# Planning TensorE ahead of ScalarE's next scores, with VectorE's tiles placed by a table, in a fused attention and routed-MLP kernel

## The chip, the cores and the metric

The kernel runs on one core of one Trainium2 chip. The metric is the device time of one execution in microseconds. Before is given by three timed runs, and by one profiled execution of which page and trace are quoted.

## The reference

An attention layer with 16 query heads and one key and value head, then a layer that routes 8 of the 2048 tokens through a gated MLP. D is 448, a head 28 wide, the MLP 1792.

```python
x = A_x                                    # (1, 2048, 448), bfloat16
h = x + attention(layernorm(x))            # q = x wq, k = x wk, v = x wv, softmax(q k / sqrt(28)) v wo
n = layernorm(h)
r = n @ w_r; idx = top 8 of r              # over the 2048 tokens
y = (silu(n[idx] @ w_gate) * (n[idx] @ w_up)) @ w_down * sigmoid(r[idx])
return h + n + scatter(y, idx)
```

## The kernel before

**Blocks and tiles.** The attention is cut into 16 blocks: block b is query block b // 4 (512 queries) for the four heads of group b % 4. Each block has 16 key tiles j of 128 keys. A tile has 4 x 512 x 128 scores, in two halves p of two heads. One half is a *score pair*: two 64-row matmuls side by side on TensorE (`qk`, ps<-Q,K), into two PSUM banks of 512 columns.

**Two ways to the exponential.** Most tiles are ScalarE's (`act_unit`): the score pair goes to banks 0 and 1 or 2 and 3 in turn, and one ACTIVATE of 128 x 1024 (line L982) writes P, a ring of six places. Four matmuls with the values (`act_pv`, ps<-P,Vs, the *value product*) then use two places, that is one tile. The other tiles are VectorE's (`dve_unit`): the pair goes to banks 4 and 5, a clamp to integers (L994) makes the bits of a bfloat16, and after both halves three shifted copies of the tile (`shift`, L1001) give, with four scaled sets of values, a finer exponential; each of the four has its own value product (`dve_pv`, ps<-Y,Vs). A shift takes either VectorE or, for tiles in `shared`, its third one GpSimd. 63 of the 256 tiles are VectorE's.

**Banks.** Block b adds its value products up in bank 6 + b % 2. The other of banks 6 and 7 serves, during block b, the query projection of block b + 2 (`q_project`, ps<-xnT,wq_pad, then a copy to Q) and the rows of the output projection (`out_proj`, ps<-wo_pad,On). When a block is done, VectorE copies the bank to Ot (`post_block`, L715); only then may block b + 2 begin its value products there, and block b + 1's projections use it. The sums of the softmax then go through DRAM for a reciprocal, and GpSimd makes On.

**Start and end.** The tokens come in four chunks of 512. `chunk0` and `chunk` normalize, transpose (ps<-ident,xn) and project keys and values; blocks 0 and 1 run interleaved while the later chunks are made. `late_consts` fills constants that are needed later, on GpSimd. After the last exponential come the last block's division, the last four rows of 128 tokens, the choice of the 8 tokens and their MLP.

**What sets the order.** All work is first recorded as operations with an engine, an estimated duration, dependencies and a priority (`_Graph.op`). `_Graph.plan` then plays the engines on a time line of these estimates: each engine takes, of its operations that are ready, the one with the lowest priority number, and if none is ready the one that will be ready first. The resulting orders are emitted as they are, with semaphores; on the chip each engine works through its own in that order. Priorities are places in the sequence of blocks, 16 to a block: ScalarE's score pairs get `t - 3`, VectorE's `t - 2.9`, chunk c `8 * c - 3`. VectorE's tiles per block come from short hand-made lists (`where`, `LD`, `FD`), the shared shifts from `PN`, and the query projections stand at 6.5 sixteenths of each block.

Of the kernel before, what the change touches and what calls it, by code (L numbers as in the profile page):

```python
# [15 lines left out]

PE, AC, DV, PO, SP = "pe", "act", "dve", "pool", "sp"


class _Op:  # L20
    __slots__ = ("eng", "fns", "dur", "lat", "deps", "prio", "idx", "dma", "start", "end", "sig", "name", "nsucc",
                 "pred_left", "succs", "ready", "form", "lock")


class _Graph:
# [16 lines left out]
    def op(self, eng, fns, dur, reads=(), writes=(), prio=None, dma=False, acc=False, name="", form=0,  # L42
           after=(), lock=False):
        o = _Op()
# [7 lines left out]
        o.form = form  # L52
        o.lock = (lock or eng == PO) and not dma
# [30 lines left out]
    def plan(self):  # L84
# [180 lines left out]
def _main(nc, G, sb, ps, psb, flag, scr, xs, ptab, A_x, A_wq, A_wk, A_wv, A_wo, B_w_r, B_w_gate, B_w_up, B_w_down, out,  # L265
# [156 lines left out]
    dma(wk_sb[0:CK, :, :], A_wk.rearrange("(k p) n -> p k n", p=CK), ["wk_sb"], lat=4450.0)  # L422
    dma(wq_sb[0:CK, :, 0:CK], wq_v[:, :, 0:CK], [("wq", 0)], lat=5300.0)
    dma(wv_sb[0:CK, :, :], A_wv.rearrange("(k p) n -> p k n", p=CK), ["wv_sb"], lat=5700.0)
    dma(wq_sb[0:CK, :, CK:D], wq_v[:, :, CK:D], [("wq", 1)], lat=6400.0)
# [25 lines left out]
    def pad_wq(g, after=()):  # L451
# [5 lines left out]
        else:  # L457
# [39 lines left out]
    def late_consts(gate):  # L497
        G.prio = -400
        G.op(PO, lambda e: e.tensor_copy(wv_pad[0:CK, :, 1:1 + DH], wv_sb[0:CK, :, :]), 250,
             reads=["wv_sb", "wv_pad"], writes=["wv_pad"], after=gate)  # L500
# [5 lines left out]
        for i in range(4):  # L506
# [13 lines left out]
        G.op(PO, lambda e: e.iota(iota_i[:, 0, 0:4], [[128, 4]], base=8, channel_multiplier=1), 140, writes=["iota_i"], after=gate)  # L520
        G.op(PO, lambda e: e.iota(iota_i[:, 0, 4:5], [[0, 1]], base=0, channel_multiplier=1), 140, writes=["iota_i"], after=gate)
        G.op(PO, lambda e: e.tensor_copy(iota_n[:, :], iota_i[:, 0, 0:5]), 200, reads=["iota_i"], writes=["iota_n"])
        G.op(PO, lambda e: e.iota(iota_i[:, 1, 0:1], [[0, 1]], base=0, channel_multiplier=128), 140, writes=["iota_j"], after=gate)
        G.op(PO, lambda e: e.tensor_copy(p128[:, :], iota_i[:, 1, 0:1]), 200, reads=["iota_j"], writes=["p128"])
        G.op(PO, lambda e: e.iota(idi[0:8, 0:96], [[1, 96]], base=0, channel_multiplier=0), 250, writes=["idi"], after=gate)
        G.op(PO, lambda e: e.tensor_copy(iota96[:, :], idi[0:8, 0:96]), 300, reads=["idi"], writes=["iota96"])
        G.op(PO, lambda e: e.iota(iota_i[:, 0, :], [[256, NT // 2], [0, 2]], base=0, channel_multiplier=0), 140,
             writes=["iota_i"], after=gate)
        G.op(PO, lambda e: e.iota(iota_i[:, 1, :], [[0, NT // 2], [128, 2]], base=0, channel_multiplier=1), 140,
             writes=["iota_i", "iota_j"], after=gate)  # L530
# [3 lines left out]
        G.op(PO, lambda e: e.iota(idi[:, :], [[-32, 4], [0, 32]], base=0, channel_multiplier=1), 250, writes=["idi"], after=gate)  # L534
# [782 lines left out]
```

## Time and profile before

| | |
|---|---|
| three timed runs | 393.46 us median, 392.99 to 394.96 |
| the profiled execution | 392.07 us, its span 390.2 us |
| busiest engines | ScalarE 375.1 us, TensorE 348.8, VectorE 344.1, GpSimd 117.2 |
| moved by DMA | 17.12 MB in all, 44 GB/s |

The page's busy shares are averages. With several engines near 90% it is the holes in the row of one engine, and what stands ahead of the late instruction, that tell the bound; the timeline and the chain show these. Matmul ends in the trace are modelled, so starts are the safer numbers. "PE" is TensorE, "DVE" VectorE, "ACT" ScalarE, "POOL" GpSimd, and all TensorE matmuls but transposes have one line (L400), so that they are told apart by their tiles.

### The profile page before, as it was taken

To read this page: it belongs to the slowest core of one execution; us is meant where nothing else is said; L and a number is where in the kernel's file an instruction comes from. 1 tells how busy PE (TensorE), PEld (TensorE's weight loads), DVE (VectorE), ACT (ScalarE), POOL (GpSimd) and SP (SyncE) were. 2 spreads that over 40 slices of the span, in tenths; PEclk is the share of its full clock that TensorE was granted. 3 is DMA by queue.
4 is the path that set the end of the run, shared out by engine and by line. 5 is a ranking of instruction groups with operands and counts; after the bars stand their busy time and mean duration, and the time that the engine had idled before them with its cause. 6 is when DMAs were issued, how large, how long until landed. Compare 5 with 4: busy or idle time off the path is not lost.

```text
span 390.2 us, 8159 instructions
## 1 busy us (share of the span) xinstructions
PE 348.8 (89%) x3373; PEld 108.8 (28%) x3373; DVE 344.1 (88%) x617; ACT 375.1 (96%) x431; POOL 117.2 (30%) x150
## 2 busy tenths in 40 slices
PE   8899889999888998989988999999898998999945
PEld 7344222222222222222222222222222222222225
DVE  6985879999998999989998999988999998999482
ACT  6999989999999999999999999999999999999992
POOL 7440000540145020444145342543402254212100
PEclk9899999999999999999999999999999999999985
DMA  8696000100000000010102000010102010111011
GB/s 210 157 235 185 2 2 1 46 16 26 5 7 25 3 28 27 30 47 16 40 6 73 2 29 27 29 47 17 41 3 77 3 52 26 40 37 34 0 50 54
DMA packets 18045, 17.12 MB, mean 44 GB/s; under 512 B 6660, under 2 KB 15124, under 8 KB 18004
## 3 DMA queue, kind: packets, MB, share of 16 engines
q1 hardware_dynamic: 17652, 16.32, 14.5%
q8 instruction: 27, 0.44, 0.5%
q10 hardware_dynamic: 288, 0.23, 0.2%
q14 instruction: 14, 0.11, 0.1%
q0 software_dynamic: 64, 0.02, 0.0%
HBM read 11.70 MB, written 4.86 MB: 42 GB/s over the span
## 4 chain that ended last, share of the span: by engine, by line
ACT 74%; PE 19%; DVE 5%; issue 1%; POOL 0%; POOLq 0%
ACT P L982 73%; PE ps L400 18%; DVE Y L994 2%; DVE Y L1001 1%; ACT xn L928 1%; PE ps L403 1%; DVE bn L898 0%; ACT x_sb L789 0%; POOL out_dram L1209 0%; ACT Rb L705 0%; ACT Rb L703 0%; DVE Ot L715 0%; POOL ident L430 0%; DVE On L709 0%; ACT wq_sb L1206 0%
## 5 line engine op out<-in xcount | busy, mean ns | idle before, releaser
L982 ACT ACTIVATE P<-ps 128x1024 bf16<-128x1024 f32 x386 | 357.1, 1093 | 4.8 <-PE ps L400 3.9
L400 PE MATMUL ps<-Q,K 64*128 64x512 bf16 x1024 | 181.7, 386 | 28.1 <-ACT P L982 20.4
L994 DVE TENSOR_SCALAR Y<-ps 128x1024 int16<-128x1024 f32 x126 | 153.2, 1216 | 16.4 <-PE ps L400 15.8
L1001 DVE TENSOR_SCALAR Y<-Y 128x2048 int16<-128x2048 int16 x155 | 104.9, 702 | 0.6
L400 PEld LDWEIGHTS ps<-Q,K 64*128 64x128 bf16 x1024 | 45.0, 93 | 171.5 <-ACT P L982 132.7
L1001 POOL TENSOR_SCALAR Y<-Y 128x2048 int16<-128x2048 int16 x34 | 64.5, 1899 | 84.1 <-DVE Y L1001 78.8
L400 PE MATMUL ps<-Y,Vs 128*32 128x512 bf16 x1008 | 86.9, 383 | 0.5 <-DVE Y L1001 0.2
L400 PE MATMUL ps<-P,Vs 128*32 128x512 bf16 x772 | 76.4, 389 | 0.5 <-DVE Vs L487 0.3
L400 PEld LDWEIGHTS ps<-Y,Vs 128*32 128x32 bf16 x1008 | 24.9, 95 | 31.2 <-issue 18.9
L400 PEld LDWEIGHTS ps<-P,Vs 128*32 128x32 bf16 x772 | 19.8, 93 | 42.3 <-issue 40.5
L731 POOL TENSOR_TENSOR On<-Ot,Rb 128x512 bf16<-128x512 f32 x15 | 19.1, 1272 | 36.1 <-DVE Y L1001 16.3
L727 POOL TENSOR_TENSOR Ls<-Ls,Lc 128x16 f32<-128x16 f32 x15 | 3.3, 220 | 77.3 <-DVE Y L1001 59.6
L400 PE MATMUL ps<-xnT,wq_pad 112*128 112x512 bf16 (+1 forms) x68 | 18.7, 371 | 0.4 <-DVE Ot L715 0.4
L400 PE MATMUL ps<-wo_pad,On 128*128 128x448 bf16 (+1 forms) x64 | 17.0, 358 | 1.5 <-DVE On L709 1.3
L479 DVE TENSOR_SCALAR Q<-ps,qone 128x512 bf16<-128x512 f32 x15 | 11.1, 737 | 2.4 <-PE ps L400 2.4
L759 POOL TENSOR_TENSOR hbuf<-st,nhalf 128x1 f32<-128x1 f32 x12 | 7.5, 627 | 17.6 <-DVE Y L1001 10.9
L715 DVE COPY Ot<-ps 128x512 f32<-128x512 f32 x15 | 10.2, 683 | 1.1 <-PE ps L400 0.8
L725 POOL TENSOR_TENSOR Lsi<-Lsi,Li 128x16 f32<-128x16 f32 x15 | 4.0, 266 | 17.1 <-DVE Y L1001 11.8
L753 DVE TENSOR_TENSOR hbuf<-ps,x_sb 128x448 f32<-128x448 f32 x12 | 7.4, 618 | 1.0 <-PE ps L400 0.8
L1209 POOL DMA_INDIRECT out_dram<-wq_sb,idxc x1 | 0.9, 931 | 24.2 <-DVE wq_sb L1208 24.2
L768 DVE SCALAR_TENSOR_TENSOR junk<-hbuf,w_rb 128x448 bf16<-128x448 f32 x12 | 8.1, 678 | 0.0
L755 DVE BATCH_NORM_STATS2 bn<-hbuf 128x6 f32<-128x448 f32 x12 | 7.5, 623 | 0.2
(209 smaller groups left out, 174.1 us busy)
## 6 DMA issues: line engine op xcount, KB each, us to landing
Rb<-h_scr SPq DMA_DIRECT2D x15, 256.0 KB
h_scr<-hbuf SPq DMA_DIRECT2D x12, 225.0 KB, 2.2
out_dram<-x_sb SPq DMA_DIRECT2D x8, 224.0 KB, 2.1
wg_sb<-in_B_w_gate_dram SPq DMA_DIRECT2D x1, 1568.0 KB, 11.9
wu_sb<-in_B_w_up_dram SPq DMA_DIRECT2D x1, 1568.0 KB, 18.2
wd_sb<-in_B_w_down_dram SPq DMA_DIRECT2D x1, 1568.0 KB, 21.9
x_sb<-in_A_x_dram SPq DMA_DIRECT2D x3, 448.0 KB, 5.7
wo_pad<-in_A_wo_dram SPq DMA_DIRECT2D x4, 98.0 KB
```

Of the source, the lines that this page charges most:

```text
L400: return lambda e: e.matmul(o, lhsT=l, rhs=r, start=start, stop=stop)
L479: G.op(DV, lambda e: e.tensor_scalar(Q[:, b % 4, :], ps[:, bank, :], qone[:, 0:1], None, ALU.add), dvt(512), reads=[pk(bank), "qone"], wri ...
L715: G.op(DV, lambda e: e.tensor_copy(Ot[:, rb, :], ps[:, acc_bank(b), :]), dvt(512), reads=[pk(acc_bank(b))], writes=[("Ot", rb)], prio=u - 30)
L725: G.op(LE, lambda e: e.tensor_tensor(Lsi[:, :], Lsi[:, :], Li[:, rb, :], ALU.add), 150, reads=["Lsi", ("Li", rb)], writes=["Lsi"])
L731: G.op(PO, lambda e: e.tensor_tensor(On[:, qb % 2, g, :], Ot[:, rb, :], Rb[:, rb, :], ALU.mult), 1270, reads=[("Ot", rb), ("Rb", rb)], wri ...
L753: G.op(DV, lambda e: e.tensor_tensor(h, ps[:, bank, 0:D], x_sb[:, t, 0:D], ALU.add), dvt(D), reads=[pk(bank), ("x", t)], writes=[("h", hr)])
L755: G.op(DV, lambda e: e.bn_stats(bn6[:, t, :], h), dvt(D), reads=[("h", hr)], writes=[("bn6", t)])
L759: G.op(PO, lambda e: e.tensor_tensor(s4, st[:, t, 7:8], nhalf[:, 0:1], ALU.pow), 570, reads=[("st7", t), "nhalf"], writes=[("h4", hr)])
L768: G.op(DV, lambda e: e.scalar_tensor_tensor(junk[:, :], h, s4, w_rb[:, :], ALU.mult, ALU.mult, accum_out=st[:, t, 2:3]), 700, reads=[("h", ...
L982: marks["exp"] = G.op(AC, lambda e: e.activation(P[:, sl, :, :], ps[:, b0:b0 + 2, :], ACT.Exp, bias=EBIAS, scale=OCT), 905, reads=[pk(b0), ...
L994: G.op(DV, lambda e: e.tensor_scalar(Y[:, n, 0, p:p + 3:2, :].bitcast(I16), ps[:, 4:6, :], 0.0, 32639.0 - 3 * STEP, ALU.max, ALU.min), 114 ...
L1001: G.op(PO if po else DV, lambda e: e.tensor_scalar(Y[:, n, v, :, :].bitcast(I16), Y[:, n, 0, :, :].bitcast(I16), 1.0, v * STEP, ALU.mult, ...
```

## The change

The planner gets a flag `crit`, set on ScalarE's score pairs. When TensorE is about to take another operation and such a pair will be ready soon, it takes only work that ends within SLACK (248 ns) of that moment; if there is none and the pair is less than WAIT (240 ns) away, TensorE is left idle for it. The lists for VectorE's tiles are replaced by a table: per block the tiles, how many shifts go to GpSimd, and an offset of their times; four early tiles in blocks 0 and 1 (before: five); a place for each query projection, output row and chunk. 62 tiles are VectorE's. The planning latencies of four DMAs are lowered, the wv_pad copy stands with the first constants, and the iotas lose their dependence on the first chunk.

```diff
+SLACK, WAIT = 248.0, 240.0
+TILES = {
+    2: ((0, 5, 8, 13), 4, -0.95),
+    3: ((0, 3, 6, 10, 13), 3, 0.94),
...
+EARLY = [(0, 5, 18.21), (0, 15, 22.04), (0, 4, 23.54), (1, 12, 28.01)]
+QUERY = {2: 12.3, 3: 12.3, 4: 6.9, 5: 7.0, 6: 11.5, 7: 11.1, 8: 8.7, 9: 10.4, 10: 6.7, 11: 9.5, 12: 10.1, 13: 7.6}
+ROWS = {
+    (0, 0): 10.9, (0, 1): 7.3, (0, 2): 10.3, (0, 3): 9.3, (1, 0): 10.7, (1, 1): 11.9, (1, 2): 13.1,
+    (1, 3): 9.9, (2, 0): 6.2, (2, 1): 11.4, (2, 2): 8.4, (2, 3): 9.2
+}
+CHUNK = (0.0, 5.1, 10.9, 36.9)
@@ plan
                 if now:
                     c = min(now, key=lambda o: (o.prio, o.idx))
                     s = t
+                    soon = min((o for o in lst if o.crit and t < o.ready), key=lambda o: o.ready, default=None)
+                    if soon is not None and not c.crit and c.eng == PE:
+                        fit = [o for o in now if t + o.dur + 100.0 * (o.form != form) <= soon.ready + SLACK]
+                        if fit:
+                            c = min(fit, key=lambda o: (o.prio, o.idx))
+                        elif soon.ready - t < WAIT:
+                            c, s = soon, soon.ready
@@ _main
-    dma(wk_sb[0:CK, :, :], A_wk.rearrange("(k p) n -> p k n", p=CK), ["wk_sb"], lat=4450.0)
+    dma(wk_sb[0:CK, :, :], A_wk.rearrange("(k p) n -> p k n", p=CK), ["wk_sb"], lat=3300.0)
...
+    G.op(PO, lambda e: e.tensor_copy(wv_pad[0:CK, :, 1:1 + DH], wv_sb[0:CK, :, :]), 250,
+         reads=["wv_sb", "wv_pad"], writes=["wv_pad"])
@@ late_consts
-        G.op(PO, lambda e: e.tensor_copy(wv_pad[0:CK, :, 1:1 + DH], wv_sb[0:CK, :, :]), 250,
-             reads=["wv_sb", "wv_pad"], writes=["wv_pad"], after=gate)
-        G.op(PO, lambda e: e.iota(iota_i[:, 0, 0:4], [[128, 4]], base=8, channel_multiplier=1), 140, writes=["iota_i"], after=gate)
+        G.op(PO, lambda e: e.iota(iota_i[:, 0, 0:4], [[128, 4]], base=8, channel_multiplier=1), 140, writes=["iota_i"])
...
@@ chunk
-        G.prio = 8 * c - 3.0
+        G.prio = CHUNK[c]
@@ tiles
-    groups = [5 if b in (5, 10) else 3 if b in () else 4 for b in range(NB)]
-    PN = {2: 3, 4: 5, 6: 3, 7: 2, 8: 5, 9: 3, 10: 5, 11: 5, 13: 5, 14: 2}
-    LD = (0, 3, 7, 10)
-    FD, FN, FT, FS = (5, 9, 13), 5, 18.5, 2.8
-    where = {0: (), 1: (9,), 2: (5, 11), 3: (3, 7, 11), 4: (1, 5, 9, 13), 5: (1, 4, 7, 10, 13)}
...
-        d = where[groups[b]] if b < NB - 1 else LD
+        d, _, dt = TILES[b]
         for j in range(NT):
             if j in d:
-                dve_tiles.append((b, j, 16.0 * b + j - 0.5))
+                dve_tiles.append((b, j, 16.0 * b + j - 0.5 + dt))
...
-    shared = {m for m, (b, j, t) in enumerate(dve_tiles) if rank[m] < PN.get(b, 0)}
+    shared = {m for m, (b, j, t) in enumerate(dve_tiles) if b in TILES and rank[m] < TILES[b][1]}
...
         G.op(PE, qk(b0, b, j, p), 216, reads=[("Q", b % 4), ("Qh", b % 4), kk(j, p)], writes=[pk(b0), pk(b0 + 1)],
-             prio=t - 3, form=1)
+             prio=t - 3, form=1, crit=True)
...
-            at(16 * b + 6.5, q_project, b + 2, misc_bank(b))
+            at(16 * b + QUERY[b], q_project, b + 2, misc_bank(b))
...
-                    at(16 * ln_block(b // 4, k) + (9.5 if b < 11 else 4.5 + 6.0 * (k % 2)), out_proj, b // 4, k)
+                    at(16 * ln_block(b // 4, k) + ROWS[b // 4, k], out_proj, b // 4, k)
```

What this does to TensorE's order at two places. First the start of block 2, where blocks 0 and 1 end. Before, in TensorE's order (Q,K are score pairs, Y,Vs and P,Vs value products of VectorE's and ScalarE's tiles, xnT,wq_pad block 3's query projection):

```order
124 L400 MATMUL ps<-Q,K 128x512 x4
125 L400 MATMUL ps<-xnT,wq_pad 128x512 x2
126 L400 MATMUL ps<-Q,K 128x512 x2
127 L400 MATMUL ps<-Y,Vs 32x512 x4
128 L400 MATMUL ps<-Q,K 128x512 x2
129 L400 MATMUL ps<-xnT,wq_pad 128x512 x2
130 L400 MATMUL ps<-Q,K 128x512 x4
131 L400 MATMUL ps<-P,Vs 32x512 x12
132 L400 MATMUL ps<-Y,Vs 32x512 x8
```

Row 131 is the first value product of block 2, which waits for block 0's Ot copy; rows 126, 128 and the second pair of 130 are ScalarE's. The same place after, where the value products of ScalarE's last tiles of block 1 are row 116 and block 2's first is row 118:

```order
113 L436 MATMUL ps<-Q,K 128x512 x8
114 L436 MATMUL ps<-Y,Vs 32x512 x8
115 L436 MATMUL ps<-Q,K 128x512 x2
116 L436 MATMUL ps<-P,Vs 32x512 x8
117 L436 MATMUL ps<-Q,K 128x512 x6
118 L436 MATMUL ps<-P,Vs 32x512 x4
119 L436 MATMUL ps<-Y,Vs 32x512 x8
120 L436 MATMUL ps<-Q,K 128x512 x2
121 L436 MATMUL ps<-xnT,wq_pad 128x512 x2
```

The value product of block 2's first ScalarE tile has moved from behind the scores of ScalarE's fourth tile of the block to behind those of the second, and block 3's projection from ahead of it to behind it. Block 0's last VectorE value product, row 127 before, is further up in the order after.

Second, block 8, where block 10's queries are projected. TensorE's order before (ScalarE's score pairs are both of row 389, rows 393 and 395 and the second pair of 397; row 391 and the first pair of 397 are VectorE's; wo_pad,On is an output row):

```order
389 L400 MATMUL ps<-Q,K 128x512 x4
390 L400 MATMUL ps<-P,Vs 32x512 x4
391 L400 MATMUL ps<-Q,K 128x512 x2
392 L400 MATMUL ps<-xnT,wq_pad 128x512 x2
393 L400 MATMUL ps<-Q,K 128x512 x2
394 L400 MATMUL ps<-xnT,wq_pad 128x512 x2
395 L400 MATMUL ps<-Q,K 128x512 x2
396 L400 MATMUL ps<-P,Vs 32x512 x4
397 L400 MATMUL ps<-Q,K 128x512 x4
398 L400 MATMUL ps<-wo_pad,On 128x448 x4
```

After, at the same place (ScalarE's are the first pair of row 396, rows 398, 400 and 404, and the second pair of 402):

```order
396 L436 MATMUL ps<-Q,K 128x512 x4
397 L436 MATMUL ps<-P,Vs 32x512 x4
398 L436 MATMUL ps<-Q,K 128x512 x2
399 L436 MATMUL ps<-xnT,wq_pad 128x512 x2
400 L436 MATMUL ps<-Q,K 128x512 x2
401 L436 MATMUL ps<-P,Vs 32x512 x4
402 L436 MATMUL ps<-Q,K 128x512 x4
403 L436 MATMUL ps<-xnT,wq_pad 128x512 x2
404 L436 MATMUL ps<-Q,K 128x512 x2
```

Between ScalarE's pairs there stands now either half a projection, or a value product with a VectorE pair, not both, and the output row has left this place for a later one.

More of the change, by code (lines that the diff above doesn't have):

```diff
@@ L943, in _main @@
     evs = []
-    groups = [5 if b in (5, 10) else 3 if b in () else 4 for b in range(NB)]
-    PN = {2: 3, 4: 5, 6: 3, 7: 2, 8: 5, 9: 3, 10: 5, 11: 5, 13: 5, 14: 2}
-    LD = (0, 3, 7, 10)
-    FD, FN, FT, FS = (5, 9, 13), 5, 18.5, 2.8
-    where = {0: (), 1: (9,), 2: (5, 11), 3: (3, 7, 11), 4: (1, 5, 9, 13), 5: (1, 4, 7, 10, 13)}
     dve_tiles, act_tiles = [], []
     first = [(b, j) for c in range(4) for b in range(2) for j in range(4 * c, 4 * c + 4)]
-    early = [(b, j) for j in FD for b in range(2)][:FN]
-    for n, (b, j) in enumerate(early):
-        dve_tiles.append((b, j, FT + FS * n))
-    left = [p for p in first if p not in early]
+    for b, j, t in EARLY:
+        dve_tiles.append((b, j, t))
+    left = [p for p in first if p not in [q[0:2] for q in EARLY]]
     for n, (b, j) in enumerate(left):
```

36 lines of the change are left out of this document (25 added, 11 removed).

## The prediction

> **What bounds the kernel now.** I read the page first: the busy shares, the chain that ended last, and the costliest group.
>
> ```profile
> span 390.2 us, 8159 instructions
> ...
> PE 348.8 (89%) x3373; PEld 108.8 (28%) x3373; DVE 344.1 (88%) x617; ACT 375.1 (96%) x431; POOL 117.2 (30%) x150
> ...
> ACT 74%; PE 19%; DVE 5%; issue 1%; POOL 0%; POOLq 0%
> ...
> L982 ACT ACTIVATE P<-ps 128x1024 bf16<-128x1024 f32 x386 | 357.1, 1093 | 4.8 <-PE ps L400 3.9
> ```
>
> ScalarE is busy for 96% of the span, 357.1 us of it with 386 exponentials of one shape (called exps below). The chain is ScalarE's for 74%; the 19% of TensorE in it are stretches in which scores were issued just in time. So the question is how close the row of exps is to a row without holes. Next comes ScalarE's timeline over the exps.
>
> ```profile
> 9.73 9.38 ACT L982 ACTIVATE P<-ps 128x1024 bf16<-128x1024 f32 x10 [1.25 <-PE ps L400]
> 19.65 35.44 ACT L982 ACTIVATE P<-ps 128x1024 bf16<-128x1024 f32 x38 [0.55 <-PE ps L400]
> 55.95 11.59 ACT L982 ACTIVATE P<-ps 128x1024 bf16<-128x1024 f32 x12 [0.86 <-PE ps L400]
> 68.58 129.43 ACT L982 ACTIVATE P<-ps 128x1024 bf16<-128x1024 f32 x140 [1.04 <-PE ps L400]
> 198.18 172.24 ACT L982 ACTIVATE P<-ps 128x1024 bf16<-128x1024 f32 x186 [0.16 <-PE ps L400]
> 370.31 1.40 ACT L789 ACTIVATE x_sb<-hbuf,st 128x448 bf16<-128x448 f32 x2
> ```
>
> The exps run from 9.73 to 198.18 + 172.24 = 370.42 with nothing else between: 360.7 us. Exps overlap by a little, so the 1093 ns that one takes isn't the pace. I take the pace from two stretches of the same timeline without a hole.
>
> ```profile
> 95.47 36.80 ACT L982 ACTIVATE P<-ps 128x1024 bf16<-128x1024 f32 x40
> 231.65 16.66 ACT L982 ACTIVATE P<-ps 128x1024 bf16<-128x1024 f32 x18
> ```
>
> 22 more exps take 20.14 us more: 0.9155 us each. 386 exps without a hole would take 385 x 0.9155 + 1.09 = 353.6 us, so the stretch loses 360.7 - 353.6 = **7.1 us**. Of that 0.55 + 0.86 + 1.04 + 0.16 = 2.6 show as idle time; the rest are exps that start late by less than their overlap. Before the stretch lie 9.73 us, behind it 390.2 - 370.4 = 19.8 us. The 7.1 us are all that a better order can win inside the stretch.
>
> **What the losses are.** There are three kinds. First, the block boundary, in the mixed timeline around 68 us:
>
> ```profile
> 66.73 0.39 PE L400 MATMUL ps<-Q,K 64*128 64x512 bf16 x2
> 67.06 0.61 PE L400 MATMUL ps<-xnT,wq_pad 112*128 112x512 bf16 x2
> 67.14 0.68 DVE L715 COPY Ot<-ps 128x512 f32<-128x512 f32 x1
> 67.60 0.61 PE L400 MATMUL ps<-Q,K 64*128 64x512 bf16 x4
> 68.13 0.83 PE L400 MATMUL ps<-P,Vs 128*32 128x512 bf16 x12
> ```
>
> The exp that starts at 68.58 had its scores at 67.12. What it lacked was a place in P: P has six, and the place is free only when the value product of the exp six before it has run, which stands at 68.13, behind two exps' score pairs too many, because block 2's first value product needs block 0's bank, copied at 67.14. The exp at 55.95 has the same cause. I counted this in the order of before: four value products stand behind the scores of the exp that needs their place, for the 49th, 51st, 55th and 61st exp. In the changed order there is none. Second, the transposes of the second chunk:
>
> ```profile
> 17.86 1.43 PE L403 MATMUL ps<-ident,xn 128*112 128x128 bf16 x12
> 19.22 0.39 PE L400 MATMUL ps<-Q,K 64*128 64x512 bf16 x2
> ```
>
> Twelve wait for VectorE's xn, and the score pair behind them comes at 19.22, which gives the idle 0.55. Third, bursts on TensorE, here in block 8:
>
> ```profile
> 196.24 0.39 PE L400 MATMUL ps<-Q,K 64*128 64x512 bf16 x2 [0.53 <-ACT P L982]
> 196.56 0.40 PE L400 MATMUL ps<-P,Vs 128*32 128x512 bf16 x4
> 196.89 0.39 PE L400 MATMUL ps<-Q,K 64*128 64x512 bf16 x2
> 197.21 0.60 PE L400 MATMUL ps<-xnT,wq_pad 112*128 112x512 bf16 x2
> 197.75 0.39 PE L400 MATMUL ps<-Q,K 64*128 64x512 bf16 x2
> ```
>
> Between two of ScalarE's score pairs stand a value product, a pair for VectorE and half a projection: 197.75 - 196.24 = 1.51 us for a pace of 0.92. The exp behind it starts at 198.18 after the idle 0.16.
>
> **The change part by part.**
>
> *One tile more for ScalarE.* VectorE has 62 tiles in place of 63 (four early ones in place of five, 58 later ones in both). ScalarE gets two exps: 2 x 0.9155 = **+1.8 us**, wholly on the path. VectorE loses some 3.5 us of work, which is off it.
>
> *The planner's look-ahead.* It adds no instruction; it lets TensorE take other work only if that ends near the moment when the next of ScalarE's score pairs is ready. To see its worth I add up, along each order, TensorE's work between ScalarE's score pairs, from the rows above: 12 value matmuls take 0.83 and 4 take 0.40, so a group of four is 0.215; a change between shapes adds 0.32 - 0.215 = 0.11; half a projection is 197.75 - 197.21 - 0.11 = 0.43. What exceeds 0.92 per pair is carried on. This estimate of the backlog, set against before, puts 44 of 386 pairs over 0.4 us behind and the worst 0.95; of the 20 exps after the 80th that end over 50 ns late in the trace, 17 belong to these pairs. In the changed order 1 of 388 is over 0.4 us (0.42), and 11 are over 0.3, where before has 69. Backlog under 0.4 costs nothing that the trace shows. So the bursts, about 7.1 - 0.65 (transposes, 0.55 idle and the rest late) - 2.5 (boundary, 1.9 idle and the rest late) = 4 us, leave 0.1.
>
> *Early tiles and places of VectorE's tiles.* Block 0's last VectorE tile now comes before block 1's, so block 0's bank is copied earlier and the first value products of block 2 stand ahead of the scores that need their place: of the 2.5 us nothing need stay. In the second chunk eight transposes stand before the score pair in place of twelve: of the 0.65 I leave 0.1.
>
> *Chunk, projection and row times.* The query projections all go later (block 10's from 6.5 to 8.7 sixteenths into block 8), of the output rows some later and some earlier. Both need a bank that the block before must have given back; if that is late, TensorE waits with ScalarE's pairs queued behind it. Later is safer there, and the earlier rows stay in the middle of their blocks: 0. The last chunk's priority falls behind VectorE's first tiles, yet in the order its VectorE rows still stand ahead of them: 0.
>
> *GpSimd's copies.* The wv_pad copy now stands ahead of the late constants, behind the wk_rep copy, and the iotas lose their gate. Queued behind it are the padded wq copies that the second projection waits for. They wait for their own DMA anyway, so 0, and about 0.3 us (one small copy) if that cover is gone. One shift of Y fewer goes to GpSimd (33 for 34), off the path. The changed DMA latencies are planning numbers; the DMA order is the same at the start, and the first exp starts as before. The 19.8 us behind the last exp hold the same instructions: 0.
>
> *What no row of before shows* is what new waits of TensorE on VectorE the other order brings. From below it is 0.1 us in all (the backlog above); from above the 3 us that the stretch loses before its 62nd exp, where VectorE is fullest. I take 0.8, near the low end, since VectorE has less to do there and a later block shows how little its lateness costs (below). With 0.1 + 0.1 the stretch keeps 1.0.
>
> Sum: 387 x 0.9155 + 1.09 + 1.0 = 356.4 for 360.7, **-4.3 us**: span 385.9. The profiled execution took 392.07 for its span of 390.2, so 387.8. The runs' median, 393.46, is 1.4 above that execution: **389.2**. With 0.1 to 3.0 us kept, 388.3 to 391.2.
>
> **The clock gate.** The change makes TensorE wait on purpose.
>
> ```profile
> PE ps L400 <- ACT P L982: 20.6, 62, 0.5
> ...
> 70.00:130.00 60.00, 53.23 (x492) 14.56 (x494) 56.19 (x82) 59.88 (x66) 19.94 (x19) 1.00 0.06 20
> ...
> 370.00:390.00 20.00, 10.14 (x244) 7.38 (x240) 10.83 (x56) 12.29 (x30) 0.93 (x1) 0.69 0.16 51
> ```
>
> TensorE's waits on exps are up to 0.5 us long already, at a granted clock of 1.00; at the end, busy for half the time, it is granted 0.69. The look-ahead holds TensorE for 0.24 us at most (its WAIT), so I expect 1.00.
> The Trainium skill ("TensorE: Matmul & The Clock Gate", A second HAM failure mode: psum-queue depth-cycling) says otherwise: short idle times between groups of matmuls, while banks are cycled, can make the clock swing between half and full. By that rule the change would be a loss; in the window of 70 to 130 us the trace does not bear it out.
>
> **The rivals.**
>
> *Holes elsewhere (12%).* TensorE's order is fixed for a planned timeline; where VectorE or a DMA is later than planned, a score pair waits behind them. For it: TensorE has one queue and more rows in it now wait where they didn't. Against it: nearly all late exps of the trace are explained by the order alone, without a late VectorE; and that the change does what it says is seen in the order. Four boundaries at the 0.86 to 1.04 us seen, and the rest kept, make about 5.3 us of losses, 1.8 less than now, which the two exps eat: 393.5, no change.
>
> *VectorE becomes the bound in blocks of five tiles (8%, the slower side).*
>
> ```profile
> 9.70:370.50 360.80, 331.12 (x3050) 94.57 (x3048) 326.84 (x538) 357.21 (x387) 108.99 (x115) 1.00 0.14 39
> ...
> 58.97 1.13 DVE Y L994
> 60.10 1.20 DVE Y L1001 x2
> ...
> 131.09 19.94 ACT L982 ACTIVATE P<-ps 128x1024 bf16<-128x1024 f32 x21
> ```
>
> A tile is two clamps and three shifts, 2 x 1.13 + 3 x 0.60 = 4.1 us. VectorE is busy for 91% of the stretch, 20 us of a four-tile block's 24 exps (22 us). A fifth tile makes it 24 against 22 exps in 20.1: 3.9 too much. Before has two such blocks (5 and 10), after four (3, 7, 10, 13). If a block can't pass its excess on, two more cost 7.8 us, and 389.2 becomes 397. Against it speaks the last row, inside block 5: 21 exps in 19.94, where 20 x 0.9155 + 1.09 = 19.4; the excess cost 0.5 us, not 3.9. It decides if PE's waits on L994's line grow past some 5 us.
>
> *The clock falls (2%).* TensorE's work per exp by the sum above is 0.78 us, some 0.24 of it changes of shape; at half clock the rest doubles: 1.3 us, 0.4 over the pace. A twentieth of the exps in such spells costs 7.8 us: 397.
>
> **How the numbers follow.** The forecast has 78%, the rivals 12, 8 and 2. A measurement tells 0.5% (2 us) from no change; all of the forecast's 388.3 to 391.2 lies below 391.5, the first rival within, the others above. The range takes the forecast's ends and widens them by the runs' spread (392.99 to 394.96 around 393.46), 0.7 below and 1.0 above: 387.6 to 392.2; it leaves out most of the rivals.
>
> **What would show it.** In the profile after, the exps' row on ScalarE's timeline should be 388 long in about 356.4 us with the idle 0.86 and 1.04 at the start of block 2 gone, and no piece of some 0.16 in block 8; the pace stays at 0.9155. The first exp should start at about 9.7, and about 19.8 us follow the last. It is wrong if the stretch keeps over 3 us of losses, if TensorE's waits on VectorE pass 5 us, if the clock between 70 and 370 us is below 1.00, or if the time behind the last exp grows.

## The result and the profile after

The changed kernel takes 388.31 us (median of four runs, 387.67 to 389.16), the kernel before 393.23 (four runs, the three above among them, 392.50 to 394.96): ratio 0.9882, 95% interval 0.9854 to 0.9910. That is 1.2% faster, and clear of the spread. A second set of six runs gave 388.58 us and 0.9892 (0.9868 to 0.9916). The prediction was 389.2, faster. The profiled execution took 387.67 us, its span is 385.9; the forecast had 387.8 and 385.9.

From the page of the kernel after, the span, the engines' busy time, the chain by engine, and the exponentials' group:

```profile
span 385.9 us, 8129 instructions
...
PE 344.0 (89%) x3361; PEld 105.6 (27%) x3361; DVE 338.2 (88%) x613; ACT 374.1 (97%) x433; POOL 115.0 (30%) x149
...
ACT 92%; PE 3%; DVE 3%; DMA 1%; issue 0%; SPq 0%; POOL 0%; POOLq 0%
...
L1012 ACT ACTIVATE P<-ps 128x1024 bf16<-128x1024 f32 x388 | 356.3, 1132 | 1.4 <-PE ps L436 1.3
```

The chain that ended last was ScalarE's for 74%, TensorE's for 19%; now it is ScalarE's for 92%. ScalarE's busy time is slightly less than before though it has two exps more: an exp that starts late overlaps less with the one before it, and such exps are gone. ScalarE's timeline over the exps of the kernel after, and the same view of a shorter window:

```profile
9.47 356.41 ACT L1012 ACTIVATE P<-ps 128x1024 bf16<-128x1024 f32 x388 [1.29 <-PE ps L436]
365.72 1.41 ACT L825 ACTIVATE x_sb<-hbuf,st 128x448 bf16<-128x448 f32 x2
...
199.24 101.22 ACT L1012 ACTIVATE P<-ps 128x1024 bf16<-128x1024 f32 x110
```

The five pieces of before have become one row of 388 exps, 356.41 us long (forecast: 356.4). By the prediction's pace it loses 356.41 - (387 x 0.9155 + 1.09) = 1.02 us, where before lost 7.1. The short window has (101.22 - 1.09) / 109 = 0.9186 us for each exp, the whole row (356.41 - 1.09) / 387 = 0.9181. No idle piece is left. Measured from end to end in the trace, 381 of the 387 exps follow within 25 ns of 0.9155 us, 0.4 us over it in all; six end later, by 0.65 us together. Over half of that, 0.18 and 0.17 us, is at exps 370 and 371, the first at 348.19 us. TensorE's row just ahead of them:

```profile
347.55 0.61 PE L436 MATMUL ps<-Q,K 64*128 64x512 bf16 x4 [0.74 <-DVE Y L1024]
```

VectorE's pair, the first of the row, waits there 0.74 us for a clamp, and ScalarE's pair is queued behind it.

TensorE's rows in block 8 of the kernel after, the second place of the order:

```profile
194.07 0.39 PE L436 MATMUL ps<-Q,K 64*128 64x512 bf16 x2
194.40 0.61 PE L436 MATMUL ps<-xnT,wq_pad 112*128 112x512 bf16 x2
194.97 0.39 PE L436 MATMUL ps<-Q,K 64*128 64x512 bf16 x2
195.29 0.40 PE L436 MATMUL ps<-P,Vs 128*32 128x512 bf16 x4
195.62 0.66 PE L436 MATMUL ps<-Q,K 64*128 64x512 bf16 x4
196.21 0.61 PE L436 MATMUL ps<-xnT,wq_pad 112*128 112x512 bf16 x2
196.81 0.39 PE L436 MATMUL ps<-Q,K 64*128 64x512 bf16 x2
```

ScalarE's pairs at 194.07 and 194.97 start 0.90 us apart, and from there to the one at 196.81, with one between in the row at 195.62, it is 1.84 us for two. Before had 1.51 for one. The windows of the kernel after (the third number from the end is the granted clock):

```profile
70.00:130.00 60.00, 54.12 (x520) 14.97 (x518) 53.33 (x79) 60.00 (x67) 21.43 (x16) 1.00 0.05 15
9.70:370.50 360.80, 328.82 (x3044) 92.33 (x3044) 324.38 (x546) 360.54 (x399) 106.74 (x116) 1.00 0.14 40
370.00:390.00 20.00, 7.50 (x227) 6.52 (x227) 7.76 (x46) 7.82 (x20) 0.93 (x1) 0.64 0.12 39
```

TensorE's waits on exps and on VectorE's clamp, after (us in total, times, longest):

```profile
PE ps L436 <- ACT P L1012: 25.0, 77, 0.5
...
PE ps L436 <- DVE Y L1024: 1.5, 4, 0.7
```

and on the clamp before:

```profile
PE ps L400 <- DVE Y L994: 2.7, 10, 0.5
```

TensorE waits more for ScalarE (25.0 us for 20.6) and less for VectorE: it now more often stands ready when a bank comes free.

### The profile page after: what moved, and what is told of

It is laid out like the page before. It is cut to its first block, busy times and chain, and to the rows that moved or that the text cites. A ratio compares the mean times of both kernels' runs of the same rounds, so it can differ in the third digit from the quotient of the medians.

```text
span 385.9 us, 8129 instructions
## 1 busy us (share of the span) xinstructions
PE 344.0 (89%) x3361; PEld 105.6 (27%) x3361; DVE 338.2 (88%) x613; ACT 374.1 (97%) x433; POOL 115.0 (30%) x149
## 4 chain that ended last, share of the span: by engine, by line
ACT 92%; PE 3%; DVE 3%; DMA 1%; issue 0%; SPq 0%; POOL 0%; POOLq 0%
ACT P L1012 90%; PE ps L436 3%; DMA wq_sb<-in_A_wq_dram 1%; ACT xn L964 1%; DVE Y L1024 1%; DVE topb L856 0%; DVE bn L934 0%; SPq L449 0%; ACT x_sb L825 0%; DVE Y L1031 0%; ACT xnT L618 0%; POOL out_dram L1239 0%; ACT Rb L741 0%; ACT Rb L739 0%; ACT wq_pad L491 0%
## 5 line engine op out<-in xcount | busy, mean ns | idle before, releaser
L436 PE MATMUL ps<-Q,K 64*128 64x512 bf16 x1024 | 179.9, 385 | 29.3 <-ACT P L1012 25.0
L1024 DVE TENSOR_SCALAR Y<-ps 128x1024 int16<-128x1024 f32 x124 | 151.2, 1219 | 19.8 <-PE ps L436 19.5
L1031 DVE TENSOR_SCALAR Y<-Y 128x2048 int16<-128x2048 int16 x153 | 100.4, 685 | 0.5
L1031 POOL TENSOR_SCALAR Y<-Y 128x2048 int16<-128x2048 int16 x33 | 62.6, 1898 | 96.4 <-DVE Y L1031 87.6
L436 PE MATMUL ps<-Y,Vs 128*32 128x512 bf16 x992 | 84.9, 383 | 0.0
L436 PEld LDWEIGHTS ps<-Y,Vs 128*32 128x32 bf16 x992 | 23.8, 95 | 27.3 <-issue 17.5
L763 POOL TENSOR_TENSOR Ls<-Ls,Lc 128x16 f32<-128x16 f32 x15 | 4.2, 280 | 68.2 <-DVE Y L1031 60.9
L795 POOL TENSOR_TENSOR hbuf<-st,nhalf 128x1 f32<-128x1 f32 x12 | 6.6, 552 | 14.3 <-DVE Y L1031 10.3
L719 DVE TENSOR_SCALAR K<-ps,ksc,kb 128x512 bf16<-128x512 f32 x6 | 4.6, 803 | 3.3 <-PE ps L436 3.3
```

Of the source, the lines that this page charges most:

```text
L436: return lambda e: e.matmul(o, lhsT=l, rhs=r, start=start, stop=stop)
L719: G.op(DV, lambda e, bank=bank, c=c, p=p: e.tensor_scalar(K[:, p, c * 512:(c + 1) * 512], ps[:, bank, :], ksc[:, p:p + 1], kb[:, p:p + 1], ...
L795: G.op(PO, lambda e: e.tensor_tensor(s4, st[:, t, 7:8], nhalf[:, 0:1], ALU.pow), 570, reads=[("st7", t), "nhalf"], writes=[("h4", hr)])
L1024: G.op(DV, lambda e: e.tensor_scalar(Y[:, n, 0, p:p + 3:2, :].bitcast(I16), ps[:, 4:6, :], 0.0, 32639.0 - 3 * STEP, ALU.max, ALU.min), 114 ...
L1031: G.op(PO if po else DV, lambda e: e.tensor_scalar(Y[:, n, v, :, :].bitcast(I16), Y[:, n, 0, :, :].bitcast(I16), 1.0, v * STEP, ALU.mult, ...
```

## The experiments

The theory was the prediction's: along TensorE's order, the work between ScalarE's score pairs (the backlog) and the value products that stand behind the scores that need their place (late places) settle how much the row of exps loses. "Lost" below is the row's length less (n - 1) x 0.9155 + 1.09, from each profile; where single exps are called late or a hole is given in us, it is by how much the end comes over 0.9155 us behind the end of the exp before. The counts are made in the planned order, and do not come from the chip. The kernels were timed in several sets, between which the median of before moves from 392.7 to 393.7, so a difference of medians across sets is good to about 0.5 us; the ratio is to before in the same set.

| kernel | median us | ratio (95%) | exps | lost us | pairs over 0.4 us behind | late places |
|---|---|---|---|---|---|---|
| before | 392.7 to 393.7 | 1 | 386 | 7.1 | 44 | 4 |
| changed | 388.31 | 0.9882 (0.9854 to 0.9910) | 388 | 1.0 | 1 | 0 |
| look-ahead alone | 398.19 | 1.0106 (1.0062 to 1.0150) | 386 | 11.8 | 50 | 11 |
| changed, no look-ahead | 391.42 | 0.9944 (0.9917 to 0.9971) | 388 | 4.1 | 22 | 1 |
| changed, no hold | 390.55 | 0.9932 (0.9908 to 0.9956) | 388 | 3.2 | 24 | 0 |
| changed, old query places | 392.41 | 0.9979 (0.9956 to 1.0001) | 388 | 5.0 | 23 | 8 |
| early tiles alone | 393.01 | 0.9974 (0.9950 to 0.9998) | 388 | 4.9 | 32 | 0 |

**The look-ahead alone**, put into the kernel before with nothing else.

```diff
-                 prio=t - 3, form=1)
+                 prio=t - 3, form=1, crit=True)
...
+                    soon = min((o for o in lst if o.crit and t < o.ready), key=lambda o: o.ready, default=None)
```

> The kernel before with the planner's look-ahead and nothing else of the change (63 VectorE tiles, old places). Order theory: the time is the pace of the exps plus what the order makes them lose, and the look-ahead is worth only what the order that comes out is worth. This order has 50 of 386 score pairs over 0.4 us of TensorE backlog (before 44), 30 over 0.6 us (before 12) and 11 value products behind the scores that need their place in P (before 4). So it loses some 10 us in place of 7: about 396.5 us, slower than before by 2 to 5. Look-ahead rival: the look-ahead removes the bursts of about 4 us wherever it is put: about 389. Load rival: the gain comes from the table that takes a tile from VectorE, the look-ahead does little: 392.5 to 394.

398.19 us, slower than before by 1.06% (0.62 to 1.50). The row of exps loses 11.8 us. The counted late places are for exps 49, 51, 61, 153, 279, 285, 299, 361, 371 and 375 and one more; the profile has a hole of 0.2 to 1.7 us at each of these ten, 8.5 us together. TensorE's and ScalarE's rows of this run at exp 49:

```profile
54.10 0.60 PE L409 MATMUL ps<-Q,K 64*128 64x512 bf16 x4 [0.53 <-ACT P L991]
...
54.64 0.69 PE L409 MATMUL ps<-Y,Vs 128*32 128x512 bf16 x8
...
55.15 0.39 PE L409 MATMUL ps<-P,Vs 128*32 128x512 bf16 x4
55.59 1.94 ACT L991 ACTIVATE P<-ps 128x1024 bf16<-128x1024 f32 x2 [1.54 <-PE ps L409]
```

The scores are in the row at 54.10, done by 54.70; ScalarE starts after the value product of 55.15, which frees the place in P. The look-ahead protects only score pairs. Without new places for the tiles it lets the value products run late, and they hold ScalarE just as well. One hole has another cause, the prediction's first rival, once: at 85.33 TensorE waits 0.89 us for a shift that GpSimd makes, with a score pair queued behind.

```profile
85.33 0.40 PE L409 MATMUL ps<-Y,Vs 128*32 128x512 bf16 x4 [0.89 <-POOL Y L1010]
85.66 0.39 PE L409 MATMUL ps<-Q,K 64*128 64x512 bf16 x2
```

So the look-ahead is no improvement by itself; the 4 us that the prediction gives under its name are those of look-ahead and table together.

**The changed kernel without the look-ahead** (its seven lines in `plan` left out, the table kept).

```diff
-                    soon = min((o for o in lst if o.crit and t < o.ready), key=lambda o: o.ready, default=None)
...
-                            c, s = soon, soon.ready
```

> The changed kernel without the look-ahead in the planner, all tables kept. Order theory: 22 of 388 pairs over 0.4 us of backlog (after 1, before 44), 2 over 0.6, 1 late place in P: some 3 to 4 us lost in place of 1.0, so 390.5 to 392, that is 2.2 to 3.7 above the changed kernel; the bursts return, the holes at the start of block 2 do not. Look-ahead rival: all of the 4 us of bursts return, 392 or more. Load rival: 388 to 389, no change against the changed kernel.

391.42 us, as expected; the row loses 4.1 us, 3.1 more than in the changed kernel, and the median is 3.1 higher. Given the table, this is what the look-ahead is worth.

**No hold**: WAIT at 0, so that TensorE is never left idle on purpose, while the choice among the ready work stays.

```diff
-SLACK, WAIT = 248.0, 240.0
+SLACK, WAIT = 248.0, 0.0
```

> The changed kernel with WAIT at 0: TensorE still chooses work that ends near the next score pair, but is never left idle for one. Order theory: 24 of 388 pairs are over 0.4 us behind, 9 over 0.6 (changed kernel 1 and 0), about what the order has with no look-ahead at all: some 4 us lost in place of 1.0, about 391.5 us. Rival, that the choice of work does it and the hold is a detail: within 1 us of the changed kernel, 387.7 to 389.5.

390.55 us, 0.9 below the expected time, and 3.2 us lost: 2.2 of the 3.1 go with the holding, and by subtraction 0.9 with choosing smaller work. Leaving the engine idle up to 0.24 us is the larger part of the look-ahead.

**The old places of the query projections** in the changed kernel.

```diff
-            at(16 * b + QUERY[b], q_project, b + 2, misc_bank(b))
+            at(16 * b + 6.5, q_project, b + 2, misc_bank(b))
```

> The changed kernel with every query projection back at 6.5 sixteenths of its block, the look-ahead and all other tables kept. Order theory: 23 pairs over 0.4 us, 13 over 0.6, 8 value products behind the scores that need their place, all after the 190th exp: some 4 us lost, 391 to 392.5 us, with holes of about 1 us near exp 343. Rival, that the table's places are fine tuning and the look-ahead repairs any: within 1 us of the changed kernel. Load rival: no change, the load is the same.

392.41 us: 4.1 above the changed kernel, and not told apart from before. The largest hole, at exp 343 where two value products are counted late, in TensorE's and ScalarE's rows of this run:

```profile
326.01 0.39 PE L436 MATMUL ps<-Q,K 64*128 64x512 bf16 x2 [0.53 <-ACT P L1012]
326.33 0.40 PE L436 MATMUL ps<-P,Vs 128*32 128x512 bf16 x4
326.56 0.60 PE L436 MATMUL ps<-Y,Vs 128*32 128x512 bf16 x8
326.99 0.39 PE L436 MATMUL ps<-P,Vs 128*32 128x512 bf16 x4
...
327.43 1.02 ACT L1012 ACTIVATE P<-ps 128x1024 bf16<-128x1024 f32 x1 [1.47 <-PE ps L436]
```

The prediction put the projections' new places at 0. They add no work, but undoing them shifts everything that the planner puts around them, and eight value products come late; the table is one piece.

**One tile moved from VectorE to ScalarE** in block 11 of the changed kernel.

```diff
-    11: ((2, 4, 9, 12), 1, -0.68),
+    11: ((2, 4, 9), 1, -0.68),
```

> The changed kernel with one more tile moved from VectorE to ScalarE (block 11's last), 61 tiles for VectorE, 390 exps. Order theory: the exps run at their pace with 1.0 us lost, so a tile costs two of them whole: +1.8 us, 390.1; its order has 1 pair over 0.4 us. Load rival: VectorE's load still holds the kernel, its 4 us less pay for the two exps: 388 or less.

391.41 us (0.9937, 0.9913 to 0.9960). 390 exps, one row, 358.49 us: 2.08 more than the changed kernel's, where two exps at the pace are 1.83. So a tile costs its two exps whole, and 0.25 more is lost. The rest of the 3.1 us in the median is not accounted for by the row; in the profile it lies outside: this execution's first exp came at 10.22 (9.47 there) and 20.7 us follow the last (20.0).

**The old start** (wv_pad copy and the four planned DMA latencies; the iotas stay as changed) in the changed kernel. The first of the four latencies:

```diff
-    dma(wk_sb[0:CK, :, :], A_wk.rearrange("(k p) n -> p k n", p=CK), ["wk_sb"], lat=3300.0)
+    dma(wk_sb[0:CK, :, :], A_wk.rearrange("(k p) n -> p k n", p=CK), ["wk_sb"], lat=4450.0)
...
```

> The changed kernel with the start as before: the old planning latencies of the four DMAs, and the wv_pad copy with the late constants. The order is the same behind the first score pairs (1 pair over 0.4 us). Order theory and the prediction: no change against the changed kernel, 388 to 389, 0.3 us more at most. Rival: the earlier first exp of the changed kernel (9.47 for 9.73 us) is its start's doing, and the start is worth what the first exp moves: some 0.3 us or more.

388.72 us (0.9889, 0.9843 to 0.9934), no difference that shows. Over all profiles the first exp starts at 9.62 to 10.74 us with the new start besides the changed kernel's 9.47, and at 9.73 to 10.46 with the old one: it varies from execution to execution by more than the 0.3 us of the rival. Much of that is TensorE's clock: the trace's record of the granted clock begins where it first is full, at 4.79 us in the changed kernel's first profile and at 7.91 us in a second one (below). The same 44 matmuls at the start take, in the one and in the other:

```profile
1.88 4.00 PE L436 MATMUL ps<-ident 128*128 128x128 bf16 x44 [1.88 <-POOL ident L466]
...
1.88 4.87 PE L436 MATMUL ps<-ident 128*128 128x128 bf16 x44 [1.88 <-POOL ident L466]
```

The first exps come at 9.47 and 10.74. In the run with the old start the clock was full at 4.75 and the exp came at 9.88; there VectorE waited 0.47 us for a DMA of tokens at 4.19. One trace does not tell whether the start edits are worth anything.

**The early tiles alone**, four at the new times in the kernel before.

```diff
-    early = [(b, j) for j in FD for b in range(2)][:FN]
-    for n, (b, j) in enumerate(early):
-        dve_tiles.append((b, j, FT + FS * n))
+    EARLY = [(0, 5, 18.21), (0, 15, 22.04), (0, 4, 23.54), (1, 12, 28.01)]
+    early = [q[0:2] for q in EARLY]
+    for b, j, t in EARLY:
+        dve_tiles.append((b, j, t))
```

> The kernel before with the four early VectorE tiles of the changed kernel in place of its five, nothing else. Order theory: no value product stands behind the scores that need its place any more, so the holes before exps 49, 51, 55 and 61 go (about 2.5 us), the bursts stay (32 pairs over 0.4 us) and ScalarE pays two more exps (+1.8): about 392.5 us, 0.5 to 1.5 below before. Look-ahead rival: without look-ahead only the two exps count: 395. Load rival: 4 us less on VectorE is the cause of the gain: 389 to 390.

393.01 us, ratio 0.9974. The holes at exps 49 to 61 are gone with the late places, 2.5 us by the trace of before, as the prediction had, and two exps are added. But ScalarE's timeline has a hole of 0.87 us early on, between its tenth and eleventh exp:

```profile
10.46 9.38 ACT L983 ACTIVATE P<-ps 128x1024 bf16<-128x1024 f32 x10 [1.25 <-PE ps L400]
20.71 177.60 ACT L983 ACTIVATE P<-ps 128x1024 bf16<-128x1024 f32 x192 [0.87 <-PE ps L400]
```

It stands where before has its idle 0.55, which the prediction laid to twelve transposes. TensorE's matmuls around it tell otherwise:

```profile
16.24 0.39 PE L400 MATMUL ps<-Q,K 64*128 64x512 bf16 x2 [0.53 <-ACT P L983]
...
18.07 0.61 PE L400 MATMUL ps<-Q,K 64*128 64x512 bf16 x2 [0.31 <-ACT P L983]
```

The same pair takes 0.39 and then 0.61 us: the clock has fallen. In every trace here the granted clock changes only at whole multiples of 3.41 us after it first became full. Cut at these steps, the windows of this run (the first numbers are the step's length and TensorE's busy time, the third from the end is the granted clock):

```profile
13.78:17.19 3.41, 1.96 (x18) 0.53 (x16) 3.38 (x14) 3.41 (x5) 1.67 (x2) 1.00 0.58 135
17.19:20.61 3.42, 3.11 (x19) 1.60 (x19) 2.50 (x8) 2.66 (x3) 0.10 (x1) 0.50 0.98 265
```

and those of the profiled execution of before:

```profile
12.23:15.64 3.41, 2.02 (x16) 0.59 (x16) 3.38 (x13) 3.41 (x5) 1.21 (x3) 1.00 0.59 144
15.64:19.05 3.41, 3.17 (x21) 1.51 (x20) 2.99 (x12) 3.41 (x4) 0.81 (x2) 0.50 0.84 197
```

In the first of each two steps TensorE works on score pairs and value products of ScalarE's tiles alone and is busy for 57 to 59%; in the second it is granted half its clock. A step at half clock in the middle of the kernel is called a spell below.

**The changed kernel again**, with the further kernels below.

> The changed kernel unaltered, beside the two further tables below. Both theories: 388 exps, stretch 356.4 us, about 388.4 us, 0.988 of before.

388.58 us (387.91 to 390.61). This profiled execution, 390.61 us, has the spell: ScalarE's timeline

```profile
10.74 9.27 ACT L1012 ACTIVATE P<-ps 128x1024 bf16<-128x1024 f32 x10 [1.08 <-PE ps L436]
21.01 1.02 ACT L1012 ACTIVATE P<-ps 128x1024 bf16<-128x1024 f32 x1 [0.99 <-PE ps L436]
22.21 38.66 ACT L1012 ACTIVATE P<-ps 128x1024 bf16<-128x1024 f32 x42 [0.18 <-PE ps L436]
```

loses 2.4 us, 1.4 of them there, and the steps show why:

```profile
14.73:18.14 3.41, 2.06 (x16) 0.49 (x14) 3.34 (x13) 3.41 (x5) 1.77 (x2) 1.00 0.70 166
18.14:21.56 3.42, 3.32 (x22) 1.89 (x23) 2.23 (x7) 2.43 (x4) 0.00 (x0) 0.50 1.03 277
```

So the spell can come in the changed kernel as well, and the first profile of it had none. For an execution without a profile only its mean granted clock is on record, which is a hint and no proof: half clock at the end of the kernel counts in it too, and the profiled execution of before, with its spell, has 0.979. Of 71 runs of before 25 have 0.971 to 0.974, and these take 394.86 us in the median; the other 46 have 0.978 or more and take 392.71. A mean of 0.973 is some 21 us at half clock (an estimate, 2 x 0.027 x 393), where the execution of before in the profile has 16 and the run above 19. So those 25 runs have more half clock than any trace kept here, and what it is stays open. Of the early-tiles kernel 7 of 10 runs have 0.976 or less, of the changed one 2 of 10.

**Work for TensorE in the early holes.** Eleven matmuls that nobody reads, into a bank not yet in use, behind ScalarE's early score pairs in the early-tiles kernel; and ten in the changed one.

```diff
+    def fill(b, j, p, t):
+        G.op(PE, [mm(ps[:, 7, :], K[0:64, p, j * 128:(j + 1) * 128], Q[0:64, b % 4, :], True, True)] * 1, 216 * 1,
+             reads=[("Q", b % 4), ("Qh", b % 4), kk(j, p)], writes=[pk(7)], prio=t - 2.95, form=1)
...
+            if 1 <= 2 * n + p < 12:
+                at(t + 0.6 * p + 0.001, fill, b, j, p, t + 0.6 * p)
```

> The kernel before with the four early tiles (as in the run with early tiles only), and 11 more matmuls of 64x512 into bank 7, which is not in use then: one behind each of ScalarE's score pairs 2 to 12, so that TensorE has work in the holes between 10 and 20 us. Nothing reads them. Theory (a spell of about 3.5 us at half clock comes when TensorE is used for some 0.5 to 0.75 of the 4 us before; it costs 1 to 2 us and is what spreads the runs): no spell between 14 and 21 us, granted clock 1.00 there, mean clock of every run .979 or more, all runs at the 391.5 to 392.0 of the early-tiles kernel's runs without a spell, median 391.9. Rival (the spell has another trigger, as the transfers of the inputs, or the fill only takes time on TensorE): mean clock .976 or less in half of the runs or more, median 393.0 or above.

391.52 us (0.9949, 0.9928 to 0.9971), 1.5 less than without them and 0.95 less when each is taken against before in its own set. All twelve runs lie within 390.94 to 391.90, with a mean clock of 0.979 or more. The steps of this run's profile:

```profile
12.24:15.65 3.41, 3.41 (x24) 1.07 (x22) 3.38 (x12) 3.41 (x5) 2.20 (x9) 1.00 0.51 130
15.65:19.07 3.42, 3.07 (x33) 1.52 (x29) 2.25 (x10) 3.42 (x5) 0.74 (x2) 1.00 0.94 180
```

They lie in time where those of before's profile lie (12.23 and 15.64), with the same transfers (DMA share 0.51 and 0.94 for 0.59 and 0.84). There TensorE was busy for 2.02 us and fell to half clock; here it is busy for 3.41 and does not. So the transfers do not make the spell; TensorE's light use does.

The row of exps does not explain the gain in the runs: it is 360.03 us here and 360.25 without the matmuls. TensorE's and ScalarE's rows of this run:

```profile
17.65 0.88 PE L403 MATMUL ps<-ident,xn 128*112 128x128 bf16 x12
...
21.11 1.04 PE L400 MATMUL ps<-xnT,wk_rep 112*128 112x512 bf16 x4 [0.60 <-DVE xnT L675]
...
22.51 1.94 ACT L983 ACTIVATE P<-ps 128x1024 bf16<-128x1024 f32 x2 [0.66 <-PE ps L400]
```

At full clock the twelve transposes take 0.88 us and exp 11 is not late. But the key projection behind them now waits 0.60 us for VectorE's copy of xnT with a score pair queued behind it, and exp 14 ends 0.76 us late. So in these two executions, one with a spell and one without, the old order loses about as much, at different exps and by different causes.

> The changed kernel with 10 such matmuls, behind ScalarE's score pairs 2 to 11. Theory: the runs at 390.4 (mean clock .976) of the changed kernel no longer occur, all runs within 387.6 to 389.2, median 388.2. Rival: they occur as before (2 of 6 there), median 388.6 or above.

388.50 us (0.9870, 0.9837 to 0.9903), all six runs within 387.97 to 388.90. The two upper runs of the changed kernel do not recur, but six runs without, against two of ten, settle nothing here, and the median stays.

**One tile more on VectorE**: a further table, found by playing the planned order with durations from the traces, 63 tiles on VectorE and so 386 exps, WAIT 1040, SLACK 265.

```diff
-    9: ((5, 7, 12), 3, 0.03),
...
-    15: ((0, 4, 8, 10), 1, 0.33),
+    9: ((1, 7, 14), 2, 0.79),
...
+    15: ((0, 4, 6, 8, 11), 3, 0.05),
```

> The changed kernel with other numbers in its tables, found by playing the planned order with durations of the traces: 63 tiles on VectorE (386 exps), in a row of which TensorE's backlog exceeds 0.3 us at 1 exp (max 0.38), with no value product behind the scores that need its place. WAIT is 1040 and SLACK 265. Theory (the order alone sets the losses): two exps fewer at 0.9155 us, losses again about 1 us, stretch 354.6, so 1.8 us below the changed kernel: 386.6 us. Rival (63 tiles are what VectorE can't serve in time, and the planned order is late there): losses of 3 us or more, 388.6 us or above, and TensorE's waits on VectorE's clamp over 15 us.

388.09 us, ratio 0.9887 (0.9852 to 0.9922): not told apart from the changed kernel, and 1.5 above what was expected. The row of exps is 355.02 us, 1.4 shorter (0.4 of the expected 1.8 is lost again); but some 20.9 us follow its last exp, 1.0 more, and this execution's first exp came at 10.41. ScalarE's first row of the final output, in this run and then in the changed kernel's:

```profile
369.27 0.54 ACT L926 ACTIVATE Ot<-ps 128x448 f32<-128x448 f32 x1 [1.06 <-PE ps L436]
```

```profile
368.66 0.54 ACT L926 ACTIVATE Ot<-ps 128x448 f32<-128x448 f32 x1
```

That is 3.84 us behind the last exp at 365.43, against 2.78 behind 365.88. Five VectorE tiles in the last block keep TensorE on value products to the end; output rows that it does ahead of the last exp in the changed kernel come behind it here. Some 1.0 us of the gain is given back at the end. A second table of the same search, also with 63 tiles, has no measured time.

> The table with 63 tiles on VectorE, with the same 10 matmuls: one tile more on VectorE and no spell. Theory: 387.7 us, 0.5 below the changed kernel as measured without the fill, and no run at 391. Rival: as without the fill, 388.1 with one run in six at 391.6.

This is the same table with the ten matmuls: 387.82 us (386.99 to 390.03), ratio 0.9872 (0.9831 to 0.9912), a row of 354.57 us with 1.0 lost. Two of its six runs take 389.86 and 390.03, so the ten matmuls do not end the spread. It is the lowest median, but the intervals overlap throughout: no version here is shown to beat the changed kernel.

## Why the prediction was right, and where it was not

**The sum: right, with some luck.** The row of exps went from 360.7 to 356.4 us, as worked out. The first exp came 0.26 us earlier and the time behind the last is 0.1 to 0.2 longer; the two nearly cancel. The luck is in the pair of executions: before's profile has a spell and the changed kernel's first one has none. With a spell in both the row goes from 360.69 to 357.79, 2.9 us in place of 4.3. The medians, 393.23 and 388.31, do not hang on that one pair.

**One tile more for ScalarE: right.** The run with yet another tile on ScalarE has a row 2.08 us longer, for 1.83 worked out.

**Losses by order: right, with a limit.** Where the count has almost nothing (the changed kernel, the old start, the one with a tile less, the further table with and without the matmuls) the rows lose 1.0 to 1.6 us, or 2.4 with a spell, elsewhere 3 to 12; in the look-ahead's own run it names ten of the fifteen holes over 0.2 us one by one. The backlog alone is no price: 23 pairs over 0.4 us go with 5.0 us in one kernel, which has eight late places too, and 24 with 3.2 in another, which has none.

**The look-ahead's share: wrong as a part.** The sum's 4 us for bursts stand under the look-ahead, and the places in the table under 0. Alone the look-ahead costs 4.5 us; in the table it is worth 3.1, and undoing the places of the projections alone costs 4.1. The count had been made of the changed order, that is of both together.

**The 0.65 us of the transposes: wrong step, size about right by luck.** Exp 11 of before ended 0.65 us late in a spell of half clock: twelve transposes took 1.43 us there and 0.88 at full clock, with exp 11 in time (the early-tiles kernel with the matmuls). Yet that run loses 0.76 at exp 14, by the wait for VectorE's copy. The changed order has the transposes and the key projection in smaller pieces, and without a spell none of its first 46 exps ends late. So against that run it wins about 0.7 us there, by another cause than the one named; what before itself loses there without a spell is on no trace. With a spell in both it wins nothing there: the repeated changed kernel loses 1.4 us at exps 11 and 12.

**VectorE: the place was wrong, the size small.** Of the 0.8 us put aside for waits of TensorE on VectorE, 0.35 came, at exps 370 and 371 in the last block; TensorE's waits on the clamp fell from 2.7 to 1.5 us. Another 0.3 of the 1.0 kept are four late exps, and 0.4 a pace of 0.9167 in place of 0.9155. The upper bound, what the stretch of before loses ahead of its 62nd exp, is 3.9 us by the trace and not 3; it was not needed. No exp in the five-tile blocks is late by 0.1 us: they bound nothing.

**The clock gate: nothing from the holding, but not absent.** From 70 to 370 us the clock stayed 1.00; TensorE waited for ScalarE 77 times in the whole span, up to 0.5 us each. The loss by the depth-cycling rule did not show. The same page of the Trainium skill ("TensorE: Matmul & The Clock Gate", What's actually happening) says that the clock is either half or full, set by how busy the engine was over a window of 3.4 us that runs free of the kernel. Here the spells last 3.41 us at 0.50, start at whole steps of that length, and strike some executions of the same kernel and not others, which agrees. The same section of the Trainium skill lets the clock fall after an idle window; here a window with 57 to 60% use was low enough.

**The step from the profile to the runs: 0.8 us too much.** The 1.4 us between before's profile and its median were added to the forecast of 387.8 as if they belonged to any kernel; the changed kernel's median lies 0.6 above its own profile. What the 1.4 are stays open. A spell as in the profile is not the cause, for that execution of before had one; the 25 runs of before with a mean clock of 0.971 to 0.974 have more half clock than that, and no trace of one is kept. Of 53 runs of the changed kernel and the five kernels that undo or alter one thing in it, none is as low, and three have 0.975 or 0.976. That the changed order makes such runs rarer is likely, but was not tested by itself.

## What to carry to other kernels

On an engine that runs a fixed order, count along it what stands between the items that the bound engine waits for, and also where the work stands that frees the bound engine's buffers; the two together find the holes before a run does. A rule that protects one of the two alone can lose, so rule and places have to be chosen together, with the rule in force. Before a hole is laid to the instructions around it, compare their durations with those of the same shape elsewhere and look at the granted clock there; a profile is one execution, and its clock may not be that of the next.

## What was not expected of the hardware

A spell of half clock on TensorE, one step of 3.41 us, came in the middle of a kernel that keeps the engine busy at 89%. The exps at it end 0.65, 0.97 and 1.4 us late in the three traces that have it. What decides is how busy TensorE is within one step of the clock, and the steps lie differently in each execution. The steps ahead of the three spells (shown above) have 57, 59 and 60%. The changed kernel's first profile has the same light stretch cut in two, and the run with the old start comes nearest without a fall:

```profile
11.61:15.02 3.41, 2.67 (x18) 0.61 (x17) 3.34 (x12) 3.41 (x5) 1.11 (x9) 1.00 0.52 137
15.02:18.44 3.42, 2.59 (x24) 1.10 (x24) 2.88 (x11) 3.42 (x5) 1.36 (x2) 1.00 0.77 177
...
14.99:18.40 3.41, 2.16 (x22) 0.87 (x21) 3.21 (x11) 3.41 (x5) 1.69 (x2) 1.00 0.88 131
```

These have 78, 76 and 63%, and full clock after them. Over the fourteen traces there are some 1500 steps at full clock. Of the 18 with 60% or less, 17 are followed by half clock; the one that is not has 57%, at 366.60 in the changed kernel's first profile. None of those with 62% or more is. Busy times are the profile's, with modelled ends, so the border is an estimate from these traces.

Eleven matmuls of 0.2 us in that stretch left no such step in the profiled run, and none of its twelve runs has a mean clock of 0.976 or less, where 7 of 10 had without them.
